# The tail of an attention-and-spectral-mixing kernel: first four output units with products, row copies and PSUM banks in another order

## The chip, the cores and the metric

The kernel runs on one core of a Trainium2 chip. The metric is the device time of one execution in microseconds (us). The profile names the engines PE (TensorE products; PEld its weight loads), DVE (VectorE), ACT (ScalarE), POOL (GpSimd) and SP (SyncE, which here only issues transfers). Sixteen DMA engines move the data; POOL and SP each feed them through a queue of their own.

## What is computed

Windowed attention with a linear bias gives x (8 batches, 576 tokens, 512 features). Then 64 Fourier modes of x along the tokens are each multiplied by a 512x512 complex matrix, the result is transformed back and added, and a rectified projection is added to that:

```python
x = np.ascontiguousarray(attn_out.transpose(0, 2, 1, 3)).reshape(B, S, H * D)
X = np.fft.rfft(x, axis=1)
Xr, Xi = (np.real(X[:, :n_modes]), np.imag(X[:, :n_modes]))
Yr = np.einsum('bmd,mde->bme', Xr, w_r) - np.einsum('bmd,mde->bme', Xi, w_i)
Yi = np.einsum('bmd,mde->bme', Xr, w_i) + np.einsum('bmd,mde->bme', Xi, w_r)
Y[:, :n_modes] = Yr + 1j * Yi
y = np.fft.irfft(Y, n=S, axis=1)
u = x + y
return (u + np.maximum(u @ w_ch, 0.0)).astype(np.float32)
```

The output is 8 x 576 x 512 in fp32, 9.44 MB.

## The kernel before, in words

The kernel has a manual schedule: each engine runs its instructions in the order in which the program issues them. Attention comes first, then a long loop over the weights of the modes (four modes to a group, 16 groups; lines 886 and 491 are its products and loads). While weights stream in, side work is done for each output unit: its tokens times w_ch are kept in `XW`, and the contribution of the early modes is added both to `XW` and to the tokens in `x`.

An output unit is a pair of batches and 128 tokens: units 0 to 3 are batches 0 and 1 at token blocks 0 to 3, units 4 to 7 batches 2 and 3, unit 8 the last 64 tokens of batches 0 to 3; units 9 to 17 do the same for batches 4 to 7. Each unit has two sides, n = 0 and 1, of 512 columns.

The change lies in the tail, after the last weights. For each unit four things happen:

- the w_ch product (tile `mm`): PE restores `XW` into PSUM (`begin` and `restore`, line 762, or 758 for the tail tokens) and adds the late modes times w_ch from `ZW` (`channels`, line 659 or 772);
- ACT rectifies it into `r` (`activate`, line 802);
- the token product (tile `yy`): PE restores the tokens from `x` and adds the late modes from `Z` (`add_tokens`, `finish_tokens`, the same lines);
- DVE adds the two into `o` (`finish`, line 842), and SP writes `o` out (line 844, or 851 for the tail tokens).

The last four modes come last of all. Their rows reach PSUM as `acc` and `pa`, ACT and DVE copy them into `yq` (lines 960 and 588), they are transposed (line 962) and multiplied by w_ch (line 601), and ACT copies that into `yw`, which lies in the memory of `F` (line 603). Units 0 and 1 take these rows directly from `yq` and `yw` through the matrix `FM` (`last_rows`, line 786). All other units read them from `Z` and `ZW`, into which small transfers copy them row by row, a batch at a time (`patch`, line 648): "token rows" go from `yq` to `Z`, "w_ch rows" from `yw` to `ZW`. In the profile the second kind reads `ZW<-F`.

Unit 0 is finished by `finish_first`: for each side, PE adds the last rows to `mm`, DVE rectifies it and adds the copy of `yy` that ACT has put into `o` (`with_tokens`, line 816), all in one instruction (line 823), and SP writes the side out (line 825).

PSUM has two slots, each with one `mm` and one `yy` tile of two banks. The lists `idle` and `free` say which slot's `mm` and `yy` may be taken next. A tile is one unit of synchronisation: whoever writes any part of a tile waits for the last reader of that tile, of either side.

The order of the end is written out by hand:

```python
finish_first(first)
activate(1)
finish(1)
activate(2)
for j in range(3, len(units)):
    activate(j)
    finish(j - 1)
finish(len(units) - 1)
```

so that on PE the w_ch product of unit j stands ahead of the token product of unit j-1.

Of the kernel before, what the change touches and what calls it, by code (L numbers as in the profile page):

```python
# [20 lines left out]
P = 128  # L21
# [391 lines left out]
def kernel(  # L413
# [22 lines left out]
    ident = const.tile([P, P], BF16, name="ident")  # L436
# [64 lines left out]
    with ExitStack() as actx:  # L501
        at = _Attention(tc, actx, q, k, v, (ident, F, FT), x, XC, raw)
        n = len(at.units)
# [10 lines left out]
        pool = _Scratch(x[:, B - 2 :].rearrange("p b t c -> p (b t c)").bitcast(FP32))  # L514
# [32 lines left out]
        for h in (0, 2):  # L547
# [4 lines left out]
        side = {0: [(at.offset, 4), (at.offset, 6), (at.decay, 5), (at.offset, 5), (at.decay, 7),  # L552
                    (at.offset, 7), (at.decay, 4), (at.decay, 6)]}
# [16 lines left out]
    with ExitStack() as mctx:  # L570
        fix = mctx.enter_context(tc.tile_pool(name="fix", bufs=1))
        YT = fix.tile([P, 2, 4, B, HM, 2], BF16, name="YT")
        pool = mctx.enter_context(tc.tile_pool(name="fin", bufs=2))
# [5 lines left out]
        lctx, pctx = ExitStack(), ExitStack()  # L579
        lps = lctx.enter_context(tc.tile_pool(name="lps", bufs=1, side="right", space=PSUM))  # L580
        ps = pctx.enter_context(tc.tile_pool(name="fps", bufs=1, space=PSUM))
        heads, free, idle = {}, [], []

        def late_end(acc):

# [38 lines left out]
        ROWS = (LO, HI)  # L624
# [19 lines left out]
        def patch(todo, rows, dst, lo=0, hi=8):  # L644

            for queue, b in todo:
                r = 64 * (b % 2) + 8 * (LAST % 8)
                queue.dma_start(out=dst(b)[r + lo : r + hi],  # L648
                                in_=rows.rearrange("(k v) e -> k v e", v=16)[lo:hi, b])
# [5 lines left out]
        def spread(dst, half, b, hf, st, tok, rows=None):  # L655

            row = ROWS[(b % 2) ^ (1 - hf)]
            rows = ZW if rows is None else rows
            nc.tensor.matmul(  # L659
                dst[ROWS[half]], lhsT=FT[row, b % 2, tokens(st, tok)], rhs=rows[row, b // 2, hf],  # L660
                start=False, stop=True, skip_group_check=True,
            )

        units = []
# [68 lines left out]
            nc.scalar.copy(src[:, 0], ys[0])  # L733
            nc.vector.tensor_copy(src[:, 1], ys[1])  # L734

        HALVES = (1, 2, len(units) - 1)
        mms, yys, rs = {}, {}, {}

        def pair(tag, slot=0):
            return heads[tag][slot].tile([P, 2, DM], FP32, tag=tag, name=tag)  # L740

        def take(j):
            slot = free.pop(0)
            yys[j] = pair("yy", slot), slot
            return yys[j][0]

        def begin(j):

            slot = idle.pop(0)
            mm = pair("mm", slot)  # L750
            mms[j] = mm, slot
            restore(mm, j, XW[:, j])

        def restore(dst, j, src):

            for n in range(2):
                if units[j][1] == FULL:
                    nc.tensor.matmul(dst[:, n], lhsT=pairs, rhs=src[:, n],
                                     start=True, stop=False, skip_group_check=True)
                    continue  # L760
                for row in range(2):
                    nc.tensor.matmul(
                        dst[ROWS[row], n], lhsT=ident[ROWS[n], ROWS[n]],
                        rhs=src[ROWS[n], row], start=True, stop=False, skip_group_check=True,
                    )

        def late_modes(dst, j, rows):

            b, st = units[j]
            for n in range(2):  # L770
                if st == FULL:
                    nc.tensor.matmul(dst[:, n], lhsT=FC, rhs=rows[:, b // 2 + n, 1],
                                     start=False, stop=True, skip_group_check=True)
                    continue
                for row in range(2):
                    spread(dst[:, n], row, b + n, 1, st, row, rows)

        def channels(j):

# [2 lines left out]
        def last_rows(ps, j, rows, sides=(0, 1)):  # L782

            st = units[j][1]
            for n in sides:
                nc.tensor.matmul(ps[:, n], lhsT=FM[:, n, st * P : (st + 1) * P], rhs=rows,
                                 start=False, stop=True, skip_group_check=True)

        def parts(j):
# [1 line left out]

        def activate(j):

            if j == 1:
                last_rows(mms[j][0], j, heads["yw"])
            else:
                begin(j)
                channels(j)
            mm, slot = mms.pop(j)
            r = rs[j] = heads["out"].tile([P, 2, DM], FP32, tag="r", name="r")  # L800
            for c in parts(j):
                nc.scalar.activation(r[:, c], mm[:, c], AF.Relu)  # L802
            idle.append(slot)

        def add_tokens(j):
# [3 lines left out]
        def finish_tokens(j):  # L809

            late_modes(yys[j][0], j, Z)

        def with_tokens(o, n):

            last_rows(yys[0][0], 0, heads["yq"], (n,))
            nc.scalar.copy(o[:, n], yys[0][0][:, n])

        def finish_first(o):

            (mm, mm_slot), (_, yy_slot) = mms.pop(0), yys[0]  # L820
            for n in range(2):
                last_rows(mm, 0, heads["yw"], (n,))
                nc.vector.scalar_tensor_tensor(out=o[:, n], in0=mm[:, n], scalar=0.0,
                                               in1=o[:, n], op0=ALU.max, op1=ALU.add)
                nc.sync.dma_start(out=out[n, :P], in_=o[:, n])
                if n == 0:
                    with_tokens(o, 1)
            del yys[0]
            idle.append(mm_slot)
            free.append(yy_slot)  # L830

        def finish(j):

            b, st = units[j]
            if j not in yys:
                take(j)
            add_tokens(j)
            finish_tokens(j)
            (yy, slot), r = yys.pop(j), rs.pop(j)
            o = heads["out"].tile([P, 2, DM], FP32, tag="o", bufs=5, name="o")  # L840
            for c in parts(j):
                nc.vector.tensor_tensor(out=o[:, c], in0=yy[:, c], in1=r[:, c], op=ALU.add)  # L842
                if st < FULL:
                    nc.sync.dma_start(
                        out=out[b + c.start : b + c.stop, st * P : (st + 1) * P].rearrange(
                            "b p e -> p b e"),
                        in_=o[:, c],
                    )
                    continue
                for n in range(c.start, c.stop):  # L850
                    nc.sync.dma_start(
                        out=out[b + 2 * n : b + 2 * n + 2, FULL * P :].rearrange("h p e -> p h e"),
                        in_=o[:, n],
                    )
            free.append(slot)

        quads, side, recycle = [], [], list(again)
        ZW = Z = XW = FM = FC = pairs = wch = w2 = None
        K1 = spot[again[-1]]
        for g in range(NM // 4):  # L860
# [5 lines left out]
            for i in range(8):  # L866
                k = 8 * g + i
                if i == 6 and g == LAST:
                    pctx.close()
                    head = mctx.enter_context(  # L870
                        tc.tile_pool(name="hps", bufs=1, space=PSUM, reuse_waits="tile"))
                    heads.update(mm=[head], yy=[head])
                    idle.append(0)
                    free.append(0)
                    begin(0)
                    channels(0)
                    take(0)
                    add_tokens(0)
                    finish_tokens(0)
                now = turns.pop(0) if turns and spot[turns[0][0]] == k else []  # L880
                for a in range(4):
                    for t in now:
# [5 lines left out]
                            lhsT=XC[:, c0 : c0 + 31 * NM + 1 : NM], rhs=wq[t][a],  # L888
# [10 lines left out]
                if k == K1:  # L899
# [64 lines left out]
            nc.vector.tensor_copy(yT[:, 2 * i : 2 * i + 2, 96:],  # L964
                                  trs[i][:, 2 * i : 2 * i + 2, 96:])
        patch([(nc.sync, 0), (nc.gpsimd, 1)], yq, lambda b: Z[:, b // 2, 1])
        patch([(nc.gpsimd, b) for b in (2, 3, 4, 5, 6)], yq, lambda b: Z[:, b // 2, 1], 6)
        yw = F[:, : DM // (2 * NM)].rearrange("p a b -> p (a b)")
        heads.update(yq=yq, yw=yw)
        first = heads["out"].tile([P, 2, DM], FP32, tag="o", bufs=5, name="o")  # L970
# [1 line left out]
        for i, c in enumerate(sides):  # L972
# [1 line left out]
            late_channels(zl, yT, yw, c)  # L974
        zctx.close()
        lctx.close()
        last = mctx.enter_context(
            tc.tile_pool(name="tps", bufs=1, side="right", space=PSUM, reuse_waits="tile"))
        heads["mm"].append(last)
        heads["yy"].append(last)  # L980
        idle.append(1)
        free.append(1)
        take(1)
        begin(1)
        channels(1)
        channel_rows = partial(patch, rows=yw, dst=lambda b: ZW[:, b // 2, 1])
        channel_rows([(nc.sync, 0), (nc.sync, 1)] + [(nc.gpsimd, b) for b in range(2, B)])
        patch([(nc.gpsimd, 7)], yq, lambda b: Z[:, b // 2, 1], 6)

        assert not side  # L990
        finish_first(first)
        activate(1)
        finish(1)
        activate(2)
        for j in range(3, len(units)):
            activate(j)
            finish(j - 1)
        finish(len(units) - 1)


# [28 lines left out]
```

## Time and profile before

| What | us |
|---|---|
| Median of three runs | 440.43 (439.67 to 441.06) |
| The profiled execution, own time | 437.99 |
| Its span, first to last instruction | 436.1 |
| Last of the weight products (line 886) starts | 402.42 |
| First sum of an output (line 823) starts | 405.90 |
| First output transfer issued (line 825) | 406.89 |
| Last sum (line 842) starts | 429.48 |

| Engine | busy us | share of the span |
|---|---|---|
| PE | 316.2 | 73% |
| DVE | 184.5 | 42% |
| ACT | 162.3 | 37% |
| POOL | 90.2 | 21% |

Busy times are sums over the whole span, and the stages have different limits; the share says little about any one of them. The profile's starts and lengths are in microseconds from the first instruction. "[0.57 <-DVE o L823]" behind an instruction means that its engine was idle for 0.57 us before it and that the event which ended the idle time was DVE's instruction of line 823 on tile `o`. Where several events were waited for, the profile names the one that came last by its inference, which is not always the true one.

### The profile page before, as it was taken

To read this page: it belongs to the slowest core of one execution; us is meant where nothing else is said; L and a number is where in the kernel's file an instruction comes from. 1 tells how busy PE (TensorE), PEld (TensorE's weight loads), DVE (VectorE), ACT (ScalarE), POOL (GpSimd) and SP (SyncE) were. 2 spreads that over 40 slices of the span, in tenths; PEclk is the share of its full clock that TensorE was granted. 3 is DMA by queue.
4 is the path that set the end of the run, shared out by engine and by line. 5 is a ranking of instruction groups with operands and counts; after the bars stand their busy time and mean duration, and the time that the engine had idled before them with its cause. 6 is when DMAs were issued, how large, how long until landed. Compare 5 with 4: busy or idle time off the path is not lost.

```text
span 436.1 us, 8292 instructions
## 1 busy us (share of the span) xinstructions
PE 316.2 (73%) x3488; PEld 177.7 (41%) x3509; DVE 184.5 (42%) x332; ACT 162.3 (37%) x211; POOL 90.2 (21%) x170
## 2 busy tenths in 40 slices
PE   5589899979686635543442487999889999788982
PEld 4367677757565312111111133444434444334430
DVE  7789799887783301000000021322213233122684
ACT  6949899988681000000000011322222322102780
POOL 8701010103424002222112110101111110012600
PEclk9969999999999955555555569999999999989997
DMA  8999999999999999999999999999999999998598
GB/s 285 326 311 310 290 316 300 307 298 299 252 217 212 215 215 213 214 214 214 215 212 214 214 215 214 215 214 215 215 214 214 215 215 215 213 215 153 190 378 311
DMA packets 50453, 105.54 MB, mean 242 GB/s; under 512 B 4032, under 2 KB 21072, under 8 KB 50416
## 3 DMA queue, kind: packets, MB, share of 16 engines
q0 software_dynamic: 19440, 68.41, 77.9%
q1 hardware_dynamic: 30976, 36.60, 25.3%
q8 instruction: 27, 0.44, 0.4%
q14 instruction: 10, 0.08, 0.1%
HBM read 162.53 MB, written 9.44 MB: 394 GB/s over the span
## 4 chain that ended last, share of the span: by engine, by line
DMA 71%; PE 10%; DVE 8%; issue 5%; POOL 2%; ACT 1%; SPq 1%; DVEq 0%; POOLq 0%; ACTq 0%
DMA w<-in_moe_w_i_dram 42%; DMA wch<-in_moe_w_ch_dram 8%; DMA qr<-in_q_dram 7%; DMA vr<-in_v_dram 6%; DVE o L842 3%; DMA qr<-in_moe_w_i_dram 3%; PE my L702 2%; DMA vr<-in_moe_w_r_dram 2%; DMA kr<-in_k_dram 2%; DVE vb L246 1%; PE acc L886 1%; PE av L344 1%; POOL Z L648 1%; PE my L659 1%; DVE att L318 1%
## 5 line engine op out<-in xcount | busy, mean ns | idle before, releaser
L886 PE MATMUL acc<-w,XC 128*32 128x512 bf16 x456 | 80.3, 478 | 68.5 <-DMA w<-in_moe_w_i_dram 34.2
L886 PEld LDWEIGHTS <-XC 128*32 128x32 bf16 x508 | 38.4, 147 | 109.2 <-issue 82.8
L307 ACT ACTIVATE att<-sc 128x1024 bf16<-128x1024 f32 x64 | 64.1, 1032 | 9.7 <-PE sc L297 9.6
L636 ACT CAST ZW<-zw 128x512 bf16<-128x512 f32 x8 | 4.7, 585 | 142.9 <-PE zw L634 142.9
L344 PE MATMUL av<-vb,att 128*128 128x132 bf16 (+1 forms) x576 | 38.4, 217 | 13.3 <-DVE x L360 8.6
L344 PEld LDWEIGHTS <-att 128*128 128x128 bf16 x704 | 36.6, 98 | 18.7 <-DVE x L360 12.0
L608 DVE TENSOR_SCALAR yq<-acc 128x512 bf16<-128x512 f32 x14 | 9.6, 687 | 81.8 <-PE acc L886 81.8
L702 PE MATMUL my<-wch,xT 128*64 128x512 bf16 x288 | 34.5, 381 | 5.7 <-ACT x L733 4.2
L711 ACT CAST XW<-my 128x512 bf16<-128x512 f32 x36 | 19.3, 589 | 50.5 <-PE my L659 50.5
L683 DVE COPY xT<-tr 128x1024 bf16<-128x1024 bf16 x18 | 12.4, 692 | 54.9 <-PE tr L681 54.9
L269 ACT COPY qkT<-tp 128x1152 bf16<-128x1152 bf16 x30 | 33.5, 1116 | 4.1 <-PE tp L263 3.6
L491 POOL DMA_DIRECT2D w<-in_moe_w_r_dram x22 | 15.6, 710 | 72.1 <-PE acc L886 46.1
L491 POOL DMA_DIRECT2D w<-in_moe_w_i_dram x23 | 16.3, 709 | 64.1 <-PE acc L886 45.3
L297 PE MATMUL sc<-qkT 64*64 64x256 bf16 (+2 forms) x640 | 25.1, 263 | 4.8 <-ACT qkT L269 1.2
L360 DVE TENSOR_TENSOR x<-av,rec 128x640 bf16<-128x640 f32 x32 | 26.4, 825 | 1.1
L702 PEld LDWEIGHTS <-xT 128*64 128x64 bf16 x288 | 17.1, 109 | 21.5 <-issue 9.1
L246 DVE CAST vb<-vr 64x1024 bf16<-64x1024 f32 x32 | 22.6, 708 | 0.2
L733 ACT CAST x<-my 128x512 bf16<-128x512 f32 x18 | 10.5, 585 | 31.6 <-PE my L659 31.6
L297 PEld LDWEIGHTS <-qkT 64*64 64x64 bf16 x640 | 14.5, 109 | 19.1 <-issue 16.0
L734 DVE CAST x<-my 128x512 bf16<-128x512 f32 x18 | 12.4, 692 | 21.7 <-PE my L659 21.7
L842 DVE TENSOR_TENSOR o<-yy,r 128x1024 f32<-128x1024 f32 (+1 forms) x20 | 20.3, 1059 | 2.1 <-ACT r L802 1.9
L318 DVE TENSOR_TENSOR att<-att,mask 128x1024 bf16<-128x1024 bf16 x32 | 20.5, 682 | 0.0
(137 smaller groups left out, 424.7 us busy)
## 6 DMA issues: line engine op xcount, KB each, us to landing
w<-in_moe_w_i_dram POOLq DMA_DIRECT2D x23, 1024.0 KB, 36.2
w<-in_moe_w_r_dram POOLq DMA_DIRECT2D x22, 1024.0 KB, 35.6
qr<-in_q_dram SPq DMA_DIRECT2D x16, 576.0 KB, 7.9
kr<-in_k_dram SPq DMA_DIRECT2D x16, 576.0 KB, 7.9
w<-in_moe_w_r_dram POOLq DMA_DIRECT2D x16, 512.0 KB, 14.2
vr<-in_v_dram SPq DMA_DIRECT2D x56, 128.0 KB, 7.6
w<-in_moe_w_i_dram POOLq DMA_DIRECT2D x13, 512.0 KB, 24.0
out_dram<-o SPq DMA_DIRECT2D x13, 512.0 KB, 5.0
```

Source lines behind the costliest of these rows:

```text
L246: nc.vector.tensor_copy(self.vb[u % 2][row, :, :, :, W * half : W * half + D], src[row, :2])
L269: (self.nc.vector.tensor_copy if u < 2 and w == "q" else self.nc.scalar.copy)(dst.rearrange("q h (p j) -> q h p j", j=TPP), tp.rearrange(" ...
L297: nc.tensor.matmul(sc[64 * half : 64 * half + 64, e, j * 256 + c0 : j * 256 + c0 + n], lhsT=qkT[row, 1, h, k0 + j : k0 + P : 2], rhs=qkT[r ...
L307: self.nc.scalar.activation(self.att[u % 2][:, kt * 8 * P : (kt + 1) * 8 * P], sc.rearrange("p e n -> p (e n)"), AF.Exp, scale=1.0 / math. ...
L318: nc.vector.tensor_tensor(out=rows, in0=rows, in1=self.table[:, heads], op=ALU.mult)
L344: nc.tensor.matmul(bank[:, qt * W : qt * W + rhs[j].shape[1]], lhsT=att[:, o : o + P], rhs=rhs[j], start=(n == 0 and j == 0), stop=(n == l ...
L360: nc.vector.tensor_tensor(out=self.x[:, b, :, cs].rearrange("p t (h d) -> p h t d", h=2), in0=tiles[:, :, :, :D], in1=rec.unsqueeze(-1).br ...
L491: nc.gpsimd.dma_start(out=t.rearrange("p s a e -> p s (a e)"), in_=w[kinds.pop()][m : m + 2].rearrange("m (p a) e -> p m (a e)", a=4))
L702: nc.tensor.matmul(mm[ROWS[half]], lhsT=lhsT, rhs=wch[:, dt], start=(dt == 0), stop=False, skip_group_check=True,)
L711: nc.scalar.copy(XW[:, j, n], mms[n])
L842: nc.vector.tensor_tensor(out=o[:, c], in0=yy[:, c], in1=r[:, c], op=ALU.add)
L886: nc.tensor.matmul(into[32 * (m % 4) : 32 * (m % 4) + 32], lhsT=XC[:, c0 : c0 + 31 * NM + 1 : NM], rhs=wq[t][a], start=(ri == 0 and a == 0 ...
```

## The change

Three things are different in the tail.

First, the PSUM tiles. The two slots are opened with a separate one-bank tile for each side (`joint` false) and serve units 0 and 1 so. After unit 0 the first slot is closed and opened again with joint tiles of two banks, and after unit 1 the second.

Second, the order. In `finish_first`, `with_tokens` of side 1 is issued ahead of the sum of side 0. In `activate(1)` the last rows are added side by side with the relus. `finish` is split into `sums` (the token product) and `finish` (the DVE sum and the write). The token products of units 1 and 2 are issued ahead of the w_ch product of unit 2; from unit 3 on, the token product of unit j follows its own w_ch product. Unit 3 is summed and written in two halves, as units 1, 2 and the last are.

Third, the row copies. SP carries the w_ch row of batch 0 only; that of batch 1 goes to POOL. POOL's order behind the token rows of batches 1 to 4 was: token rows 5, 6, w_ch rows 2 to 7, token row 7. Now it is: w_ch rows 1, 2, 3, token row 5, w_ch rows 4, 5, token rows 6, 7, w_ch rows 6, 7.

```diff
-        HALVES = (1, 2, len(units) - 1)
+        HALVES = (1, 2, 3, len(units) - 1)
...
         def pair(tag, slot=0):
-            return heads[tag][slot].tile([P, 2, DM], FP32, tag=tag, name=tag)
+            pool, joint = slots[slot]
+            if joint:
+                t = pool.tile([P, 2, DM], FP32, tag=tag, name=tag)
+                return t, t[:, 0], t[:, 1]
+            return (None, *(pool.tile([P, DM], FP32, tag=tag + str(n), name=tag)
+                            for n in range(2)))
+
+        def open_slot(slot, joint, **kw):
+            if slot in slots:
+                opened[slot].close()
+            opened[slot] = mctx.enter_context(ExitStack())
+            slots[slot] = opened[slot].enter_context(tc.tile_pool(
+                name=f"s{slot}{joint:d}", bufs=1, space=PSUM, reuse_waits="tile", **kw)), joint
+
+        def part(t, c):
+            return t[0] if c.stop - c.start == 2 else t[1 + c.start]
+
+        def whole(t, c):
+            return t if c.stop - c.start == 2 else t[:, c.start]
...
+        def hold(j):
+
+            slot = idle.pop(0)
+            mms[j] = pair("mm", slot), slot
+
         def begin(j):
 
-            slot = idle.pop(0)
-            mm = pair("mm", slot)
-            mms[j] = mm, slot
-            restore(mm, j, XW[:, j])
+            if j not in mms:
+                hold(j)
+            restore(mms[j][0], j, XW[:, j])
...
         def activate(j):
 
-            if j == 1:
-                last_rows(mms[j][0], j, heads["yw"])
-            else:
+            if j != 1:
                 begin(j)
                 channels(j)
             mm, slot = mms.pop(j)
             r = rs[j] = heads["out"].tile([P, 2, DM], FP32, tag="r", name="r")
             for c in parts(j):
-                nc.scalar.activation(r[:, c], mm[:, c], AF.Relu)
+                if j == 1:
+                    last_rows(mm, 1, heads["yw"], (c.start,))
+                nc.scalar.activation(whole(r, c), part(mm, c), AF.Relu)
             idle.append(slot)
...
                 last_rows(mm, 0, heads["yw"], (n,))
-                nc.vector.scalar_tensor_tensor(out=o[:, n], in0=mm[:, n], scalar=0.0,
+                if n == 0:
+                    with_tokens(o, 1)
+                nc.vector.scalar_tensor_tensor(out=o[:, n], in0=mm[1 + n], scalar=0.0,
                                                in1=o[:, n], op0=ALU.max, op1=ALU.add)
                 nc.sync.dma_start(out=out[n, :P], in_=o[:, n])
-                if n == 0:
-                    with_tokens(o, 1)
...
-        def finish(j):
-
-            b, st = units[j]
+        def sums(j):
+
             if j not in yys:
                 take(j)
             add_tokens(j)
             finish_tokens(j)
+
+        def finish(j):
+
+            b, st = units[j]
             (yy, slot), r = yys.pop(j), rs.pop(j)
...
-        patch([(nc.gpsimd, b) for b in (2, 3, 4, 5, 6)], yq, lambda b: Z[:, b // 2, 1], 6)
+        patch([(nc.gpsimd, b) for b in (2, 3, 4)], yq, lambda b: Z[:, b // 2, 1], 6)
...
-        channel_rows([(nc.sync, 0), (nc.sync, 1)] + [(nc.gpsimd, b) for b in range(2, B)])
-        patch([(nc.gpsimd, 7)], yq, lambda b: Z[:, b // 2, 1], 6)
+        channel_rows([(nc.sync, 0)] + [(nc.gpsimd, b) for b in (1, 2, 3)])
+        for todo in ((5,), (6, 7)):
+            patch([(nc.gpsimd, b) for b in todo], yq, lambda b: Z[:, b // 2, 1], 6)
+            channel_rows([(nc.gpsimd, b) for b in (todo[0] // 2 * 2, todo[0] // 2 * 2 + 1)])
 
         assert not side
         finish_first(first)
+        open_slot(0, True)
+        hold(2)
         activate(1)
+        sums(1)
+        sums(2)
         finish(1)
+        open_slot(1, True, side="right")
         activate(2)
+        finish(2)
+        take(3)
+        hold(3)
         for j in range(3, len(units)):
             activate(j)
-            finish(j - 1)
-        finish(len(units) - 1)
+            sums(j)
+            finish(j)
```

More of the change, by code (lines that the diff above doesn't have):

```diff
@@ L581 @@
         ps = pctx.enter_context(tc.tile_pool(name="fps", bufs=1, space=PSUM))
-        heads, free, idle = {}, [], []
+        heads, slots, opened, free, idle = {}, {}, {}, [], []
         def late_end(acc):
@@ L757, in restore @@
                 if units[j][1] == FULL:
-                    nc.tensor.matmul(dst[:, n], lhsT=pairs, rhs=src[:, n],
+                    nc.tensor.matmul(dst[1 + n], lhsT=pairs, rhs=src[:, n],
                                      start=True, stop=False, skip_group_check=True)
@@ L762, in restore @@
                     nc.tensor.matmul(
-                        dst[ROWS[row], n], lhsT=ident[ROWS[n], ROWS[n]],
+                        dst[1 + n][ROWS[row]], lhsT=ident[ROWS[n], ROWS[n]],
                         rhs=src[ROWS[n], row], start=True, stop=False, skip_group_check=True,
@@ L771, in late_modes @@
                 if st == FULL:
-                    nc.tensor.matmul(dst[:, n], lhsT=FC, rhs=rows[:, b // 2 + n, 1],
+                    nc.tensor.matmul(dst[1 + n], lhsT=FC, rhs=rows[:, b // 2 + n, 1],
                                      start=False, stop=True, skip_group_check=True)
@@ L775, in late_modes @@
                 for row in range(2):
-                    spread(dst[:, n], row, b + n, 1, st, row, rows)
+                    spread(dst[1 + n], row, b + n, 1, st, row, rows)
         def channels(j):
@@ L785, in last_rows @@
             for n in sides:
-                nc.tensor.matmul(ps[:, n], lhsT=FM[:, n, st * P : (st + 1) * P], rhs=rows,
+                nc.tensor.matmul(ps[1 + n], lhsT=FM[:, n, st * P : (st + 1) * P], rhs=rows,
                                  start=False, stop=True, skip_group_check=True)
@@ L815, in with_tokens @@
             last_rows(yys[0][0], 0, heads["yq"], (n,))
-            nc.scalar.copy(o[:, n], yys[0][0][:, n])
+            nc.scalar.copy(o[:, n], yys[0][0][1 + n])
         def finish_first(o):
@@ L841, in finish @@
             for c in parts(j):
-                nc.vector.tensor_tensor(out=o[:, c], in0=yy[:, c], in1=r[:, c], op=ALU.add)
+                nc.vector.tensor_tensor(out=whole(o, c), in0=part(yy, c), in1=whole(r, c),
+                                        op=ALU.add)
                 if st < FULL:
@@ L869 @@
                     pctx.close()
-                    head = mctx.enter_context(
-                        tc.tile_pool(name="hps", bufs=1, space=PSUM, reuse_waits="tile"))
-                    heads.update(mm=[head], yy=[head])
+                    open_slot(0, False)
                     idle.append(0)
@@ L976 @@
         lctx.close()
[L977 to L980, printed above, removed]
+        open_slot(1, False, side="right")
         idle.append(1)
```

## The prediction

> **What bounds the kernel now.** I read the coarse table by stage first: busy time in each stretch for PE, PEld, DVE, ACT and POOL, then the granted clock, the DMA share and GB/s.
>
> ```profile
> 0.00:396.00 396.00, 287.26 (x3174) 164.94 (x3193) 160.78 (x305) 142.32 (x184) 80.43 (x151) 0.85 1.06 240
> 402.80:407.80 5.00, 3.87 (x34) 1.84 (x36) 1.75 (x4) 2.77 (x7) 3.99 (x8) 1.00 0.05 10
> 407.80:413.50 5.70, 5.43 (x88) 2.65 (x87) 5.02 (x8) 5.63 (x9) 2.74 (x6) 1.00 0.88 306
> 413.50:434.00 20.50, 13.18 (x158) 5.46 (x158) 15.27 (x14) 10.99 (x12) 0.00 (x0) 0.94 1.02 378
> 434.00:436.10 2.10, 0.00 (x0) 0.00 (x0) 0.00 (x0) 0.00 (x0) 0.00 (x0) 0.50 0.06 23
> ```
>
> Until 396 the DMA engines stream weights (share 1.06); the change touches nothing there. From 402.8 to 407.8 they carry 10 GB/s: a chain of small steps makes the first output. From 413.5 to 434.0 they are full again, now with output (378 GB/s). No engine is: DVE is busy 15.3 of 20.5 us. So the end is when the last byte of 9.44 MB is written, and it moves only if writing starts earlier or has fewer holes. The half-microsecond windows show the holes, in the last column:
>
> ```profile
> 407.50:408.00 0.50, 0.50 (x12) 0.26 (x11) 0.32 (x1) 0.50 (x2) 0.50 (x2) 1.00 0.39 131
> 408.00:408.50 0.50, 0.50 (x11) 0.13 (x4) 0.38 (x1) 0.50 (x2) 0.50 (x2) 1.00 0.99 360
> 408.50:409.00 0.50, 0.37 (x8) 0.28 (x11) 0.50 (x2) 0.50 (x2) 0.50 (x2) 1.00 0.67 197
> ...
> 409.50:410.00 0.50, 0.50 (x12) 0.24 (x11) 0.21 (x1) 0.50 (x2) 0.50 (x2) 1.00 0.73 199
> ```
>
> The eleven windows from 408.0 to 413.5 read 360, 197, 365, 199, 346, 264, 281, 287, 381, 377, 307: 1.68 MB in 5.5 us. At 380 that would be 2.09 MB, so 0.41 MB or **1.07 us of writing is lost in holes**. The stretch from 405 to 408, in order of time (start, length, engine, line):
>
> ```profile
> 405.47 0.39 PE L786 MATMUL mm<-F,FM 128*128 128x512 bf16 x1
> 405.70 0.38 PE L786 MATMUL yy<-yq,FM 128*128 128x512 bf16 x1
> 405.90 0.69 DVE L823 SCALAR_TENSOR_TENSOR o<-mm,o 128x512 f32<-128x512 f32 x1 [1.83 <-DMA Z<-yq]
> 406.11 0.58 ACT L816 COPY o<-yy 128x512 f32<-128x512 f32 x1 [0.72 <-PE yy L786]
> 406.64 0.81 PE L786 MATMUL mm<-F,FM 128*128 128x512 bf16 x3 [0.57 <-DVE o L823]
> ...
> 407.13 0.69 DVE L823 SCALAR_TENSOR_TENSOR o<-mm,o 128x512 f32<-128x512 f32 x1 [0.54 <-PE mm L786]
> ```
>
> PE stands still 0.57 us for the DVE sum of side 0 before it may add side 1 of the same pair, and the second sum starts 0.54 late. SP and POOL at that time:
>
> ```profile
> 406.27 0.56 SPq L648 DMA_DIRECT2D ZW<-F  x1
> 406.89 0.44 SPq L825 DMA_DIRECT2D out_dram<-o  x1
> 406.85 0.57 POOL L648 DMA_DIRECT2D ZW<-F  x1
> ```
>
> The first sum ends at 406.59, but SP is busy with a w_ch row until 406.83, so the first output is issued at 406.89, not 406.62 (0.03 after, as with unit 1: its sum ends 409.41, its issue is at 409.44). Its bytes flow 0.9 later (131 GB/s in the window to 408.0, so from 407.8).
>
> **The change, part by part,** on the old clock. PE: 512-column products start 0.21 apart (three in 0.81 us, 0.39 each); a unit's eight 64-row products take 0.43 of PE and are done 0.63 after the first (407.38 to 408.01). DVE starts 512-wide sums 0.61 apart (408.12, 408.73) and 1024-wide ones 1.13 apart; ACT starts 512-wide relus 0.49 apart, 1024-wide ones 0.90. A 256 KB write needs 0.69 us at 380 GB/s, a 512 KB one 1.38.
>
> *Units 0 and 1, sides in their own tiles.* PE no longer waits: products of unit 0 side 1 at 405.92, unit 1 at 406.13 and 406.35. What is late next for the second sum is the ACT copy (ends 406.69): it runs 406.73 to 407.42 (was 407.13). Relus of unit 1: 406.69 and 407.18 (were 407.49, 407.98).
>
> *Token products of units 1 and 2 ahead.* Unit 1 on PE 406.57, done 407.20 (was 408.01); unit 2 from 407.00, in the cover of the wait for the second sum. Unit 1's sums: 407.45 and 408.06 (were 408.12, 408.73). Behind them stand unit 2's w_ch products, which need the second sum's bank (407.42 + 0.05) and the w_ch row of batch 1.
>
> *Row copies.* SP loses one issue (0.56), which gives the 0.27 above. POOL makes 14 issues instead of 13, 0.5 each, ending 0.5 later with nothing queued behind. Batch 1's w_ch row moves to POOL behind batch 4's token row (405.37 + 0.50), so it starts at 405.86; rows 2 and 3 at 406.4 and 406.9 (were 406.85, 407.42); batch 5's token row goes back from 405.86 to 407.4, batch 6's from 406.36 to 409.0, w_ch rows 6 and 7 by 1.0 to 410.0 and 410.5. First users of batches 4 and 5 are PE products at 415.4, of 6 and 7 at 419.9; with 3.4 us from issue to landing (the longest of the six POOL rows) the last lands at 413.9. Cost nothing; without that cover, what the row exceeds its user by. Only batch 1's row matters. Nearest rows: an 8 KB POOL row at 403.81 took 1.7 us, the one at 406.85, with output flowing, 2.4. It lands between 407.56 and 408.26; I take the middle, since output starts at 407.5. Then unit 2's products are done at 408.1 to 408.7, its relus start 408.1 to 408.7, its first sum 408.74 to 409.32 (was 409.79, which waited for its token products).
>
> By the Trainium skill, "DMA: Bandwidth & Descriptors", section Specifications, a DMA from the GpSimd queue has its first byte after about 1 us, one from sync after 0.6. By that page the row's earlier start of 0.41 is used up and unit 2 runs at the late end; my estimate of the sum is then -0.5 us. The trace has no landing time for the SP row beside it, so it neither bears this out nor excludes it.
>
> *Unit 3 in halves.* Same 512 KB; two DVE starts cost 0.09 more (2 x 0.61 against 1.13), but the first half leaves 0.6 earlier. Issues then: unit 0 at 406.62, 407.45; unit 1 408.17, 408.77; unit 2 409.46 to 410.03, then 410.07 to 410.65; unit 3 410.7 to 411.25, 411.3 to 411.85; unit 4 412.4 to 413.0 (was 413.37).
>
> *From unit 3 on, each unit's token products right behind its own w_ch products.* They need the bank that the sum of two units before frees. A loop over three units: 0.05 to PE, 0.43 token products, 0.60 next w_ch products, 0.04 to ACT, 1.02 relu, 0.02 to DVE, 1.22 sum, 3.38 us, against 3 x 1.13 = 3.39 that DVE needs alone. It hides with nothing to spare. At the two units of tail tokens (four full products, done in 1.03) it does not: DVE waits some 0.4 and 0.15 us, where it waited 0.13 and 0.26. The cover is the write queue: 1.38 us per unit against 1.13, and by 417 two units stand in it (4.2 MB issued, 3.2 moved by the windows).
>
> *Sum.* Each write reaches the engines 0.9 after issue and queues behind the last. For the old issues this gives holes of 0.27, 0.30, 0.29, 0.04, 0.31 = 1.21, against 1.07 measured. For the new: 0.14 and 0.03 before unit 1, then 0 to 0.48 before unit 2 and 0.12 to 0.21 before unit 4: 0.29 to 0.86. Gain: 0.27 earlier start + (1.07 - 0.29 to 0.86) = 1.05 to 0.48, middle 0.8, which I round up to **0.85** since the model overcounts the old holes. The profiled execution took 437.99 us: a span of 436.08 and 1.91 around it. That becomes 437.14. It lies 2.44 below the median shown; the shift moved there gives 440.43 - 0.85 = **439.6**.
>
> **Rivals.** *No holes left.* If unit 2 is on time and writes queue from the first byte, the gain is 0.27 + 1.07 = 1.34: 439.1. For it: the near-zero holes at units 1 and 3. Against: 0.14 and 0.12 stay in the working.
>
> *The row of batch 1 late.* With 2.8 us (the median of POOL's w_ch rows) it lands at 408.66 and unit 2 gains only 0.1: holes about 1.15, time -0.2. With 3.4 it lands at 409.26, unit 2's first sum starts at 410.35, the hole before it is 1.5: +0.6. So 440.2 to 441.0. For it: PE has nothing else queued that could run. Against: the long rows all ran beside output, and this one starts 1.6 us before it.
>
> *The new order in units 3 to 17 costs more than it hides: slower.* The place is the w_ch product of unit j+1 behind the token product of unit j, one unit further back than before. It decides once the loop exceeds 3 x 1.38 = 4.14 us, 0.76 over my working. That happens if the bank is freed by the previous unit's sum and not the one before: then 3.4 us bind two units, 1.7 each. Unit 4 to unit 16 from 411.5 take 13 x 1.7, unit 17's halves 1.3, issue and last write 1.6: 436.5 against the last bytes near 434.3 (82 GB/s in the window from 434.0), so +2.2: 442.6. For it: nothing to spare in my loop. Against: in the code slots alternate from unit 1 on, and the old trace has token products starting 0.05 after the sum two units before (413.34, 413.39).
>
> **How the numbers follow.** 0.3% is 1.32 us, about what a measurement of this kernel can tell from no change; the runs shown scatter by 0.7 either way. Forecast 0.48 (own range 439.0 to 440.2), no holes 0.24, late row 0.15, slower loop 0.13. Faster by over 0.3%: 0.13 of the forecast's share by scatter and 0.21 of the second's, 0.34. Slower: 0.11 of the loop's and 0.01 of the late row's, 0.12. Within: 0.54. Range 438.5 to 441.3: both ends of the hole-free and late cases with scatter, not most of the loop's.
>
> **What would show it.** First output issued near 406.6; no PE wait between the products of unit 0; unit 2's first sum near 409.0, with any wait before its w_ch products on a ZW row; holes under 0.9 us to 413.5 and then 375 to 385 GB/s to the end; last bytes at 433.4. Wrong if windows after 414 fall under 370 (the loop binds), if the row lands after 408.7, or if the span moves while writes start and fill the same.

## The result, and the profile after

The changed kernel takes 437.95 us, the median of 20 runs (436.98 to 440.09). The kernel before took 439.62 beside it (20 runs, 437.74 to 443.79). The ratio is 0.997, with a 95% interval of 0.9957 to 0.9984: 0.7 to 1.9 us less.

The two profiled executions do not show that at a glance: both have a span of 436.1 us. The reason lies ahead of the tail. The last weight product starts at 402.42 before and at 403.03 after, and with it everything behind moves 0.62 later on the clock. So all readings below count from one instruction, the ACT copy of the last four modes' rows to `yq`. Its line in the timeline of the kernel before (start, length, engine, line; in brackets the idle time before it and what ended it):

```profile
402.88 0.38 ACT L960 ACTIVATE yq<-acc 32x256 bf16<-32x256 f32 x1 [5.04 <-PE acc L886]
```

and in that of the changed kernel, where the lines are some 24 further down:

```profile
403.50 0.38 ACT L984 ACTIVATE yq<-acc 32x256 bf16<-32x256 f32 x1 [5.04 <-PE acc L910]
```

From this copy to the end of the span it is 33.22 us before and 32.60 after. (The span is printed to 0.1 us, so these two, and the "tail" below, are good to 0.05.) The stages of the changed kernel, in the columns that the prediction used (stretch, length, busy time and instructions of PE, PEld, DVE, ACT and POOL, granted clock, DMA share, GB/s):

```profile
402.80:407.80 5.00, 4.26 (x40) 2.01 (x43) 1.52 (x4) 2.95 (x8) 3.40 (x7) 1.00 0.04 9
407.80:413.50 5.70, 5.17 (x84) 2.36 (x80) 5.42 (x9) 4.80 (x9) 4.37 (x9) 1.00 0.89 309
413.50:434.00 20.50, 13.36 (x166) 5.93 (x160) 15.20 (x14) 11.96 (x13) 0.00 (x0) 0.95 1.02 378
434.00:436.10 2.10, 0.00 (x0) 0.00 (x0) 0.00 (x0) 0.00 (x0) 0.00 (x0) 0.50 0.05 19
```

The bound is the same: from 413.5 on the DMA engines are full with output at 378 GB/s, as before, and no engine is. What differs is how soon they are full. Windows of 1 us, of which the first starts 4 us after the copy, of the kernel before:

```profile
406.88:407.88 1.00, 1.00 (x13) 0.33 (x12) 0.69 (x1) 0.39 (x1) 1.00 (x2) 1.00 0.13 33
407.88:408.88 1.00, 0.87 (x20) 0.43 (x19) 0.76 (x2) 1.00 (x3) 1.00 (x3) 1.00 0.82 278
408.88:409.88 1.00, 1.00 (x20) 0.50 (x16) 0.62 (x2) 1.00 (x3) 1.00 (x3) 1.00 0.90 294
409.88:410.88 1.00, 1.00 (x24) 0.53 (x16) 1.00 (x2) 1.00 (x2) 0.66 (x2) 1.00 0.86 300
410.88:411.88 1.00, 1.00 (x24) 0.51 (x17) 1.00 (x2) 1.00 (x2) 0.00 (x0) 1.00 0.80 279
```

and of the changed kernel:

```profile
407.50:408.50 1.00, 1.00 (x24) 0.53 (x18) 1.00 (x2) 0.81 (x2) 1.00 (x3) 1.00 0.44 158
408.50:409.50 1.00, 0.99 (x20) 0.56 (x17) 0.78 (x2) 0.57 (x2) 1.00 (x3) 1.00 0.80 264
409.50:410.50 1.00, 0.89 (x16) 0.35 (x9) 0.94 (x2) 1.00 (x4) 1.00 (x2) 1.00 0.93 320
410.50:411.50 1.00, 0.79 (x16) 0.43 (x15) 1.00 (x3) 1.00 (x3) 1.00 (x3) 1.00 0.92 324
411.50:412.50 1.00, 0.86 (x19) 0.26 (x12) 1.00 (x2) 0.91 (x2) 0.67 (x2) 1.00 0.98 337
```

The last column of a 1-us window is also the number of KB moved in it; nearly all of it is output, but more than half of the 33 KB in the first row are row copies. The first row is the earlier first write (158 against 33), the last three are holes that filled up. Over the ten windows from 4 to 14 us it is 3,279 KB against 3,037; 242 KB at 380 GB/s are 0.64 us. Behind that both write at about 380 until nothing is left, and the last bytes come 31.18 us after the copy before, 30.48 after: 0.70 less. ("Last bytes" is reckoned: the end of the last full 1-us window, and what was still moved behind it at 380 GB/s.) So in these two profiles the time was won in those ten microseconds and kept.

How it was won, the timeline of the changed kernel around its first output shows:

```profile
406.09 0.39 PE L808 MATMUL mm<-F,FM 128*128 128x512 bf16 x1
406.31 0.38 PE L808 MATMUL yy<-yq,FM 128*128 128x512 bf16 x1
406.52 1.52 DVE L847 SCALAR_TENSOR_TENSOR o<-mm,o 128x512 f32<-128x512 f32 x2 [1.83 <-DMA Z<-yq]
406.53 0.81 PE L808 MATMUL mm<-F,FM 128*128 128x512 bf16 x3
406.73 0.59 ACT L838 COPY o<-yy 128x512 f32<-128x512 f32 x1 [0.72 <-PE yy L808]
...
407.24 0.37 SPq L849 DMA_DIRECT2D out_dram<-o  x1
```

PE's three further products start 0.22 after the one before, with no idle time, where the kernel before waited 0.57; DVE makes both sums in one run of 1.52, with 0.14 between them where it stood 0.54; and the first write is issued 3.74 us after the copy (407.24 - 403.50), not 4.01.

### The profile page after: what moved, and what is told of

Read it like the earlier page. It is cut to its first block, busy times and chain, and to the rows that moved or that the text cites. A ratio compares the mean times of both kernels' runs of the same rounds, so it can differ in the third digit from the quotient of the medians.

```text
span 436.1 us, 8296 instructions
## 1 busy us (share of the span) xinstructions
PE 318.1 (73%) x3488; PEld 179.3 (41%) x3509; DVE 184.8 (42%) x333; ACT 162.6 (37%) x212; POOL 92.1 (21%) x171
## 4 chain that ended last, share of the span: by engine, by line
DMA 70%; PE 11%; DVE 10%; issue 5%; SPq 1%; ACT 1%; POOL 1%; DVEq 0%; POOLq 0%; ACTq 0%
DMA w<-in_moe_w_i_dram 43%; DMA qr<-in_q_dram 9%; DMA wch<-in_moe_w_ch_dram 8%; DMA vr<-in_v_dram 6%; DMA vr<-in_moe_w_r_dram 2%; DVE vb L246 2%; PE my L702 2%; DVE o L867 2%; DVE att L318 2%; PE acc L910 1%; PE av L344 1%; PE my L659 1%; DMA out_dram<-o 1%; DVE q L251 1%; DVE x L360 1%
```

## The experiments

The theory, T in the texts, is the reading above: the tail ends when the last byte is written, and the change wins what the write queue gains before it is full. Each text names the rival that it is to be told from: that the difference is scatter between executions, that the order from unit 3 on decides, or that one part alone makes it. All nine kernels ran in five rounds beside the kernel before; the first four shared 35 of its runs, the next four another 35, the last had 16.

| Kernel | median us | before beside it | ratio, 95% interval |
|---|---|---|---|
| e1, before unchanged | 438.39 | 438.87 | 1.0001 (0.9986 to 1.0016) |
| e2, row copies only | 438.70 | 438.87 | 1.0003 (0.9987 to 1.0020) |
| e3, old row copies | 439.30 | 438.87 | 1.0017 (0.9998 to 1.0037) |
| e4, old order from unit 3 | 438.55 | 438.87 | 0.9999 (0.9984 to 1.0014) |
| e5, change unchanged | 437.93 | 438.83 | 0.998 (0.9958 to 1.0002) |
| e6, batch 1's row on SP | 438.22 | 438.83 | 0.998 (0.9964 to 0.9996) |
| e7, joint tiles | 438.77 | 438.83 | 0.9993 (0.9973 to 1.0013) |
| e8, unit 2's tokens late | 437.87 | 438.83 | 0.9981 (0.9963 to 1.0000) |
| e9, batch 4's token row later | 438.01 | 438.86 | 0.9988 (0.9969 to 1.0007) |

The second table is read from one profile of each. All times are us after the copy's start; "KB" is what was moved from 4 to 14 us; "tail" ends with the span.

| Kernel | copy at | first output issued | unit 0, 2nd sum | unit 1, 1st sum | unit 2, 1st sum | unit 4, sum | KB | last bytes | tail |
|---|---|---|---|---|---|---|---|---|---|
| before | 402.88 | 4.01 | 4.25 | 5.24 | 6.91 | 9.24 | 3037 | 31.18 | 33.22 |
| after | 403.50 | 3.74 | 3.85 | 4.49 | 6.06 | 8.46 | 3279 | 30.48 | 32.60 |
| e1 | 402.85 | 4.01 | 4.25 | 5.24 | 6.91 | 9.24 | 3041 | 31.16 | 33.45 |
| e2 | 403.65 | 3.74 | 4.25 | 5.24 | 6.91 | 9.25 | 2864 | 31.61 | 34.05 |
| e3 | 403.01 | 4.00 | 3.86 | 4.50 | 6.26 | 9.34 | 3109 | 31.12 | 33.89 |
| e4 | 403.53 | 3.74 | 3.86 | 4.50 | 6.08 | 8.97 | 3222 | 30.81 | 32.87 |
| e5 | 403.16 | 3.74 | 3.86 | 4.50 | 6.07 | 8.47 | 3268 | 30.50 | 32.64 |
| e6 | 403.51 | 4.01 | 3.86 | 4.50 | 6.24 | 8.64 | 3266 | 30.56 | 33.29 |
| e7 | 402.62 | 3.74 | 4.25 | 6.08 | 7.51 | 9.92 | 2781 | 32.21 | 34.08 |
| e8 | 402.71 | 3.74 | 3.85 | 4.49 | 6.06 | 8.46 | 3284 | 30.76 | 32.89 |
| e9 | 403.12 | 3.73 | 3.85 | 4.49 | 6.04 | 8.44 | 3232 | 30.68 | 32.68 |

The expectations of e1 to e4 count the tail from the start of the last weight product, 0.46 ahead of the copy; that gives 33.66 before and 33.05 after (33.07 in the texts).

The timed runs are coarse beside these differences: an interval of the first table is 1.3 to 1.9 us wide. They agree with the last bytes of every kernel but one: e7's loss lies outside its interval. The 0.70 of the change lies at the lower edge of its 0.7 to 1.9.

### e1: the kernel before, again

No edit.

> The kernel before, unchanged, against itself. Two clocks are read in every run of this study: the whole time, and the tail, from the start of the last weight product to the end of the span (33.66 us in the profile of before, 33.07 in that of the changed kernel). Theory T (the change shortens the tail by 0.6 us, and what the whole times differ beyond that is the scatter of the weight stream ahead of it): tail 33.6 to 33.7 again, whole time within 0.2% of itself. Rival V (the tail of before varies from execution to execution and the profile shows one of its short ones): tail over 34.0.

Measured: a ratio of 1.0001, and 33.9 by the expectation's count, between the two. The table says why: every issue and sum of the table stands where it stood, to 0.01 us, and the last bytes come at 31.16 against 31.18. Only the time from the last bytes to the end of the span differs, 2.29 against 2.04. So the tail varies by some 0.25 behind the writing, and what is written by 14 us is the better measure: 3,037 and 3,041 KB for the kernel before, and 3,279 and 3,268 for the change and its repetition in e5. The 0.64 us is far more than the two profiles of one kernel differ by.

### e2: the row copies alone

```diff
 (the kernel before, with)
-        patch([(nc.gpsimd, b) for b in (2, 3, 4, 5, 6)], ...
+        patch([(nc.gpsimd, b) for b in (2, 3, 4)], ...
-        channel_rows([(nc.sync, 0), (nc.sync, 1)] + [(nc.gpsimd, b) for b in range(2, B)])
-        patch([(nc.gpsimd, 7)], ...
+        channel_rows([(nc.sync, 0)] + [(nc.gpsimd, b) for b in (1, 2, 3)])
+        for todo in ((5,), (6, 7)):
+            patch([(nc.gpsimd, b) for b in todo], ...
+            channel_rows([(nc.gpsimd, b) for b in (todo[0] // 2 * 2, todo[0] // 2 * 2 + 1)])
```

> Before, with only the row copies in the new order (batch 1's w_ch row on the software queue, rows 2 and 3 ahead of token row 5). Theory T: the first output is issued 0.27 us earlier after the last rows are copied (3.74 against 4.01), the second sum and unit 1 stay where they were, so the first hole grows by as much; tail 33.4 to 33.6, time -0.1 to -0.3 us. Rival R (the rows are the whole gain): tail 33.0 to 33.1, time -0.6 to -1.3 us.

Measured: 1.0003, no gain, and a tail of 34.48 by the expectation's count. The first output is issued at 3.74, 0.27 earlier, as expected, and the sums stand where they stood before, but the last bytes came at 31.61, later than before. Both theories missed that. SP's own rows in e2 show where it went:

```profile
411.28 1.15 SPq L844 DMA_DIRECT2D out_dram<-o  x1
412.48 0.43 SPq L844 DMA_DIRECT2D out_dram<-o  x1
```

and so does the window behind it:

```profile
411.65:412.65 1.00, 1.00 (x24) 0.51 (x17) 1.00 (x2) 1.00 (x2) 0.68 (x2) 1.00 0.48 153
```

SP's fifth output issue took 1.15 us, and the next waited for it; with nothing in stock the writing fell to 153 GB/s. So this profile has a hole that the row copies do not explain, and its bytes cannot price them; what shows is that the earlier first write alone brought no gain. e6 tells more of what it is worth.

### e3: the new order with the old row copies

```diff
 (the changed kernel, with)
-        channel_rows([(nc.sync, 0)] + [(nc.gpsimd, b) for b in (1, 2, 3)])
...
+        channel_rows([(nc.sync, 0), (nc.sync, 1)] + [(nc.gpsimd, b) for b in range(2, B)])
+        patch([(nc.gpsimd, 7)], yq, lambda b: Z[:, b // 2, 1], 6)
```

> The changed kernel with the row copies as before (both first w_ch rows on SP, POOL's old order). Theory T: first output issued at 4.01 again, sums of units 0 to 4 otherwise as in the changed kernel except that unit 2 runs when SP's row lands; tail 33.2 to 33.4, so 0.2 to 0.4 us slower than the changed kernel and 0.3 to 0.4 faster than before. Rival R: tail 33.6, time of before.

Measured: 1.0017, and a tail of 34.35 by the expectation's count. T had 33.2 to 33.4: a miss. Units 0 and 1 are as early as in the change, yet the last bytes come at 31.12, hardly before those of the kernel before. Two rows of e3 tell:

```profile
410.86 0.40 PE L659 MATMUL mm<-ZW,FT 64*64 64x512 bf16 x2 [0.47 <-DMA ZW<-F]
...
412.35 1.23 DVE L867 TENSOR_TENSOR o<-yy,r 128x1024 f32<-128x1024 f32 x1 [0.60 <-ACT r L824]
```

Unit 4's w_ch product is now so early on PE that it stands 0.47 us waiting for a w_ch row on its way to `ZW`, and DVE waits 0.60 for it. The row is batch 3's: its issue starts 4.54 us after the copy, it lands 3.3 us later, at 7.80, and the product starts at 7.84. The first hole is the late first write (4.00), the second this one: 11 us after the copy the writing falls to 268 GB/s for a microsecond. The rows alone bring nothing (e2), and the order without them hardly anything: of the two parts neither does it alone. Which of the row copies counts, e6 shows.

### e4: the old order from unit 3 on

```diff
 (the changed kernel, with)
-        for j in range(3, len(units)):
+        activate(3)
+        for j in range(4, len(units)):
             activate(j)
-            sums(j)
-            finish(j)
+            sums(j - 1)
+            finish(j - 1)
+        sums(len(units) - 1)
+        finish(len(units) - 1)
```

> The changed kernel, but from unit 3 on with the w_ch product of unit j ahead of the token product of unit j-1, as before. Theory T (the write queue hides the order from unit 3 on): DVE waits less at the units of tail tokens, the DMA engines are full from 413 on all the same; tail 33.0 to 33.15, time within 0.1% of the changed kernel. Rival L (the new order binds in units 3 to 17): tail shorter by 0.3 us or more, 32.8 or less.

Measured: 0.9999, and a tail of 33.4 by the expectation's count, over T's 33.15 and far from the rival's 32.8. By 14 us it has moved 3,222 KB, 46 to 57 less than in e5 and the change, which is 0.12 to 0.15 us, and 185 more than before; last bytes at 30.81. By the bytes the new order from unit 3 on thus isn't the cause of most of the gain, and costs nothing, but may carry a small part (e9, with the new order, has 3,232 KB, and the timed runs do not tell e4 from the kernel before): in the old one, unit 3's token products stand behind unit 4's w_ch products, unit 3's first half waits 0.39 for them, and unit 4's sum comes at 8.97 instead of 8.46.

### e5: the change, again

No edit.

> The changed kernel again, beside the kernel before on another occasion. The clock for parts is now the start of the ACT copy of the last four modes' rows (the tail: from it to the end of the span; before 33.22 and 33.45 us in two profiles, changed 32.60). Theory T: tail 32.5 to 32.8, last full microsecond of writing about 0.7 earlier than before; whole time 0.6 to 0.9 us under before, ratio 0.998. Rival G (the tail is not all of it, the change makes typical executions faster by 1.3 us or more): ratio 0.997 or less again.

Measured: 0.998, or 0.90 us between the medians, with an interval that just reaches no change; tail 32.64, last bytes 30.50, every sum within 0.01 of the first profile. This is what T had.

### e6: batch 1's w_ch row on SP, the rest as changed

```diff
-        channel_rows([(nc.sync, 0)] + [(nc.gpsimd, b) for b in (1, 2, 3)])
+        channel_rows([(nc.sync, 0), (nc.sync, 1)] + [(nc.gpsimd, b) for b in (2, 3)])
```

> The changed kernel with batch 1's w_ch row back on SP, the rows of batches 2 and 3 staying ahead of token row 5. Theory T: first output issued 4.01 after the copy (3.74 in the changed kernel); batch 2's and 3's rows 0.5 us earlier on POOL; unit 2's first sum at 6.1 or a little earlier; no late row before unit 4 (in the kernel with all old rows it came 0.6 late). Tail 0.1 to 0.3 longer than the changed kernel, 32.7 to 32.9. Rival P (the POOL row's extra wait of 0.26 us costs what SP gains): tail as the changed kernel or shorter.

Measured: 0.998. The first output is issued at 4.01, as T had it, so the 0.27 is SP's row and nothing else. But by 14 us it has moved 3,266 KB, as much as e5, and the last bytes come at 30.56: the 0.27 is made good before the queue is full. From 5 to 8 us after the copy it moves 346, 346 and 333 KB a microsecond, where the changed kernel with its earlier start has 264, 320 and 324. That is the rival's outcome, though not for its reason, since unit 2 is summed later here, 6.24 against 6.06; the tail of 33.29, over T's 32.9, is long only because the span ends 2.73 after the last bytes. e6 and e3 differ in nothing but POOL's order: with the w_ch rows of batches 2 and 3 ahead of token rows 5 and 6, 3,266 KB against 3,109, and 0.56 us in the last bytes. So of the row copies it is those two rows, and not batch 1's, on which the gain hangs.

The row's way from SP to its user, in e6:

```profile
406.90 0.56 SPq L648 DMA_DIRECT2D ZW<-F  x1
...
409.12 0.60 ACT L824 ACTIVATE r<-mm 128x512 f32<-128x512 f32 x1 [0.79 <-PE mm L659]
```

and from POOL in the changed kernel:

```profile
406.75 0.59 POOL L648 DMA_DIRECT2D ZW<-F  x1 [0.26 <-issue]
...
408.93 0.60 ACT L824 ACTIVATE r<-mm 128x512 f32<-128x512 f32 x1 [0.62 <-PE mm L659]
```

From the start of the issue to the relu that needs the row: 2.22 us by SP, 2.18 by POOL. The DMA packets agree: the row's first 1-KB packet starts 1.21 us after the start of the issue by either way. The Trainium skill's "DMA: Bandwidth & Descriptors", section Specifications, gives the GpSimd path 0.4 us more to the first byte. For this row no such difference is seen.

### e7: joint tiles for units 0 and 1

```diff
-                    open_slot(0, False)
+                    open_slot(0, True)
...
-        open_slot(1, False, side="right")
+        open_slot(1, True, side="right")
```

> The changed kernel with joint two-bank tiles for units 0 and 1, so PE waits for the sum of side 0 again. Theory T (own tiles are what moves units 0 and 1): second sum 4.3 after the copy instead of 3.85, unit 1's first sum 5.2 instead of 4.49, holes between the first writes as before; tail 33.0 to 33.4. Rival: the later units make it up, tail within 0.1 of 32.60.

Measured: 0.9993, and the latest last bytes of all, 32.21; the tail, 34.08, is far over T's 33.0 to 33.4. The timeline of e7:

```profile
406.87 0.69 DVE L847 SCALAR_TENSOR_TENSOR o<-mm,o 128x512 f32<-128x512 f32 x1 [0.54 <-PE mm L808]
...
408.07 0.60 ACT L824 ACTIVATE r<-mm 128x512 f32<-128x512 f32 x1 [0.46 <-PE mm L808]
...
408.70 0.69 DVE L867 TENSOR_TENSOR o<-yy,r 128x512 f32<-128x512 f32 x1 [1.14 <-ACT r L824]
```

The wait of 0.54 is back, and a second one is new: the change adds the last rows of unit 1 side by side with the relus, and with one tile for both sides the product of side 1 waits for the relu of side 0. Unit 1's first sum starts at 6.08, against 5.24 before; T had 5.2, since it did not count the second wait. In the tail the tiles of their own are thus the part without which the rest is a loss: 1.71 us in the last bytes against e5, and 1.03 against the kernel before. The timed runs do not show that second loss: their interval goes from 1.2 us less than before to 0.6 more. In the profile of e7 the copy starts earlier than in any other, 0.26 ahead of the kernel before; whether its stream of weights is always shorter is not shown. The Trainium skill's "PSUM — Partial Sum Buffer", section "PSUM bank collisions raise a hardware error", asks only that two engines never be on the same bank and quadrant (32 partitions) at the same time. The trace agrees: with the sides in banks of their own PE writes side 1 from 406.53 while DVE reads side 0 from 406.52, so the wait belonged to the two-bank tile and not to the memory.

### e8: unit 2's token products behind its w_ch products

```diff
-        sums(2)
         finish(1)
         open_slot(1, True, side="right")
         activate(2)
+        sums(2)
```

> The changed kernel with unit 2's token product behind its w_ch product instead of ahead. Theory T (PE stood waiting there anyway, and unit 2's sum waits for its relu): first sum of unit 2 within 0.1 of 6.06 after the copy, tail 32.5 to 32.8. Rival (the order of the products is what fills the hole): first sum of unit 2 at 6.3 or later, tail over 32.9.

Measured: 0.9981; unit 2's first sum at 6.06, as in the change, still behind its relu (0.28). The token products of unit 2 ahead are worth nothing (3,284 KB by 14 us). The row decides when unit 2 is summed: in both kernels it lands 4.95 us after the copy and the w_ch products that need it start at 4.99. The tail is 32.89, 0.09 over T's range: the last bytes come at 30.76, 0.28 after those of the change, so single profiles differ by that much behind the point to which the parts reach.

### e9: batch 4's token row behind the w_ch rows

```diff
-        patch([(nc.gpsimd, b) for b in (2, 3, 4)], ...
+        patch([(nc.gpsimd, b) for b in (2, 3)], ...
...
-        for todo in ((5,), (6, 7)):
+        for todo in ((4, 5), (6, 7)):
```

> The changed kernel with batch 4's token row (first used by unit 9) behind the w_ch rows of batches 1 to 3. Theory T: those rows start 0.4 to 0.5 us earlier on POOL, unit 2's first sum at 5.8 after the copy instead of 6.06, the hole before it closes; last bytes 30.3 to 30.4 instead of 30.5, whole time 0.1 to 0.2 us under the changed kernel, which the timed runs can't separate. Rival: unit 2 waits for the second sum of unit 0 and not for the row, so nothing moves, first sum 6.06 again.

Measured: 0.9988, the rival's outcome, though not for its reason. With one issue less ahead of it, POOL's first w_ch row starts no earlier:

```profile
406.37 0.57 POOL L648 DMA_DIRECT2D ZW<-F  x1 [0.75 <-ACT F L603]
```

That is 3.25 us after the copy, as in the change (406.75 - 403.50). POOL's queue is not what holds it: it waits for `yw`. So this order is no faster, and nothing that ran beats the change by more than its scatter.

## Why the prediction was right and wrong

**The step that failed is the last one, "the shift moved there gives 440.43 - 0.85 = 439.6".** It hung the sum on a median of three runs. Twenty runs of the kernel before, those three among them, have a median of 439.62, and 35, 35 and 16 others have 438.87, 438.83 and 438.86. The scatter of 0.7 that the range allowed was that of the three runs around their own median, and did not hold the error of the anchor, 0.8 to 1.6. From 438.83 the same sum gives 437.98; measured beside it in e5, 437.93. From 439.62 it gives 438.77, and 437.95 was measured: half of the miss of 1.6 is the anchor, and the other half is that the two medians of twenty differ by 1.67. Nothing in the tail accounts for more than 0.70 of that; where the rest came from stays open. The profiled execution, 437.99, which the prediction set aside, lies 0.9 under the three later medians and was nearer to them than 440.43, though not to that of the twenty.

**The bound: right.** The end is when the last byte is written, at some 380 GB/s from about 414 on, in all the kernels; no engine became the bound. The forecast of 433.4 for the last bytes came out at 433.36 on the old clock, by luck: they had come at 434.06 before, not at 434.3.

**The first output: right to 0.01.** Issued at 406.62 by the forecast; 407.24 less the 0.62 by which the stream ahead ended later is 406.62. e6 shows that it is the SP row. But the sum counts these 0.27 as a gain of their own, and e6 does without them and is as far by 14 us: given the sums' times, the earlier first write seems only to move the first hole.

**Units 0 and 1: right.** The second sum was put 0.14 behind the first one's end; it starts 3.85 after the copy, 406.73 on the old clock, exactly there. Unit 1's first sum was forecast for 407.45 and came at 407.37.

**Batch 1's row: right in the sum, with an error inside.** Its issue was to start at 405.86, behind batch 4's token row, and started at 406.13: the row must wait for `yw`, and POOL's issue starts 0.74 us after ACT wrote that, while SP's row starts after 0.22. The forecast priced only POOL's queue. Then the row landed after 1.70 us, where the forecast took the middle between 1.7 and 2.4. The two errors, 0.27 and 0.35, nearly cancel: it landed at 407.83 on the old clock, and unit 2's first sum came at 408.94, inside 408.74 to 409.32. That it fits so well is luck. The sentence drawn from the Trainium skill's first-byte figures, with its -0.5, was not borne out as a mechanism (e6).

**"Only batch 1's row matters": wrong.** With rows 2 and 3 where they were, unit 4 waits 0.60 for batch 3's (e3); with them moved and batch 1's left on SP, nearly the whole gain is there (e6). The forecast worked out no user for rows 2 and 3, and for the rows behind them it took the users' old times, although it had itself moved unit 4 by 0.4 to 1.0.

**The holes: right in kind, too optimistic in size.** The forecast took the middle of 0.29 to 0.86 us and rounded the gain up, to 0.85. In the stretch that answers to its own, the change moves 327 GB/s over 5.77 us; that is 1.89 MB or 4.97 us at 380, so 0.80 is lost, near the upper end of 0.29 to 0.86, and the forecast's own sum comes to 0.27 + 1.07 - 0.80 = 0.54: the rounding went the wrong way. By the bytes moved to 14 us the gain is 0.64, by the last bytes 0.70. The timed gains cannot tell 0.64 from 0.85: e5's interval goes from no gain to 1.8, and that of the first runs, 0.7 to 1.9, has the 0.70 at its edge and the 0.64 just outside.

**The order from unit 3 on: right.** It hides. At the two units of tail tokens DVE waits 0.43 and 0.21, forecast 0.4 and 0.15, and the windows of the six microseconds from 417.5 on read 352 to 387 GB/s (348 to 389 before):

```profile
417.05 1.23 DVE L867 TENSOR_TENSOR o<-yy,r 128x1024 f32<-128x1024 f32 x1 [0.43 <-ACT r L824]
418.48 1.23 DVE L867 TENSOR_TENSOR o<-yy,r 128x1024 f32<-128x1024 f32 x1 [0.21 <-ACT r L824]
```

What the forecast did not see is that it may also bring something, 0.12 to 0.15 us by the bytes of e4, at its first units. Of the rivals, "no holes left" is out by the windows of 264 to 337 GB/s, the late row by unit 2's time, the slower loop by e4.

## What to carry to other kernels

Where a kernel ends in a full write queue, price a change by the bytes that it brings into the queue before it is full, and count from an instruction just ahead of the change, so that what varies earlier drops out. When several steps are moved earlier together, compare each transfer with the new time of its user; here neither the row copies nor the order gained measurably without the other. And hang a forecast of some tenths of a per cent on many runs: three runs of this kernel were off by 0.8 to 1.6 us, as much as the effect or more.

## What the runs showed beyond that

- At least one output issue on SP, mostly the fifth or sixth, takes 0.63 to 1.15 us instead of the 0.33 of the shortest, in every profile, 7.4 to 8.2 us after the copy. Its hole is seen where the queue is thin (e2). What causes it wasn't found.
- From the last bytes to the end of the span it is 1.9 to 2.8 us, with no relation to the kernel: 2.04 and 2.29 for the same program.
- The copy starts anywhere from 402.62 to 403.65. The two profiles of the changed kernel have it later than the two of the kernel before, but e7 and e8, which have the new rows, are the earliest, so no rule shows, and one or two profiles of a kernel are too few for one. The scatter arises in the weight stream ahead; its cause stays open, and it is as large as the effect studied here.
